# A mixing and gated feed-forward kernel on one core: reordered opening, 94-row gathers, cosines from the absolute phase, and layer 2 of the first chunk begun early

## The chip, the core and the metric

The kernel runs on one core of one Trainium2 chip. A time is the device time of one execution in microseconds (us). Of several executions the median is given, with the range or the number of runs where it matters. PE is the matmul engine, PEld its weight loads, DVE the vector engine, ACT the scalar (activation) engine, POOL the GpSimd engine, and SP the engine that issues most plain transfers.

## The reference

```python
x: (8, 3008, 256) float32            # batch, sequence, width
X = np.fft.fft(np.fft.fft(x, axis=1), axis=2).real      # mixing
t = X.reshape(24064, 256)
out = (gelu(t @ w_gate) * (t @ w_val)) @ w_out          # 256 -> 1536 -> 256, exact GELU
```

## The kernel before

The sequence of 3008 is factored into 94 x 32, and 3008 = 47 x 64 is used on the output side. For each batch the kernel adds and subtracts mirrored rows of `x` ("folds"), multiplies by a table G of cosines and sines (`s1`, into the tile A), reorders into a tile Z (`ch`, for later batches by way of device memory: SP writes `z` and reads it back), and multiplies Z by a second small table TP (`tp_e`, `tp_o`). The result is the input of the feed-forward part. It has chunks of up to 512 tokens, three for each batch. Layer 1 of a chunk takes 12 steps, one for each 128 hidden units, and I call a step a *slot*: 8 batches x 3 chunks x 12 make 288 slots. Layer 2 of a chunk is cut into 24 pieces of four matmuls, two pieces in each slot of the *next* chunk.

The mirrored rows come by gathers (indirect DMA) that POOL issues, with a column of row indices. Of 96 rows only 94 are used. Two rows have no meaning, and their index is only made legal:

```python
NP, NPX, NJ = 94, 96, 17

def cast_mirror(b, j0, nj):
    i0, o, idx = (16, 0, idx_0) if j0 == 0 else (17 - j0 - nj, 33 - j0 - nj, idx_x)
    gather(_sub(xb[b], [[1, nj * C]], (NJ + i0) * C),
           ap_replace(x, ap=[[32 * C, B * NP], [1, 32 * C]]), idx[:NPX, :], (b * T + o) * C)

def index_consts(i):                                   # idx = max(base - p, 0), by way of float32
    idx, base = ((idx_x, NP - 1), (idx_0, NP))[i]
    nc.gpsimd.iota(col_i[:, i : i + 1], pattern=[[0, 1]], base=base, channel_multiplier=-1, **IOTA)
    if i:
        nc.gpsimd.memset(col_i[0:1, i : i + 1], 0.0)
    nc.gpsimd.tensor_scalar(idx, col_i[:, i : i + 1], 0.0, None, op0=ALU.max)
```

`load_mirror` is the same for batches 2 to 7, in float32 and into the tile `x_raw`. The opening computes the tables on DVE and ACT while PE runs matmuls without use (`warm`) to raise its clock:

```python
warm(11); vec_consts(); g_phases(); vec_fills(); cw_phases()
g_sin(9, 7); g_sin_ends(); g_sin(1, 8); cw_sin()
t_columns(); t_phases(); t_sin(); warm(10)
...
fold_piece(9, 4); stage1(2); warm(4); fold_piece(13, 4); ...      # the first batch, ends in the first gate
```

And this is how a slot issues its work:

```python
pend = list(works[i // NFC - 1])           # at the first slot of a chunk: the 24 layer-2 pieces of the chunk before
...
parts["G"][fc]()                           # gate matmuls, Gelu on ACT
before[0]["g"][before[1]]()                # second gate matmul of the slot before (mirrored tokens)
parts["V"][fc]()                           # value matmul
pend.pop(0)()                              # a layer-2 piece
before[0]["v"][before[1]]()                # second value matmul; DVE and POOL write h = gelu * value
pend.pop(0)()                              # a layer-2 piece
```

POOL writes `h` for the mirrored tokens ("sign 1"), DVE for the others.

## Time and profile before

| | before |
|---|---|
| median time in the runs beside the changed kernel | 633.55 us (632.54 to 635.35, 4 runs) |
| profiled span | 632.1 us |
| first Gelu | 21.52 us |
| PE idle from 45 us on | two waits of over 0.5 us (0.63 at 52.8 us, 0.76 at 236.4 us) |

The busy table by windows, before, for 95 to 120 us (columns: length, then busy us of PE, PEld, DVE, ACT and POOL with counts, then granted clock, DMA share and GB/s):

```profile
95.00:120.00 25.00, 25.00 (x173) 16.54 (x171) 23.79 (x38) 18.00 (x35) 24.15 (x23) 1.00 0.50 132
```

PE has no idle time there at all. So a gain must come from the first slice of 16 us, or from the few waits later on. POOL is nearly as full as PE in that window (24.15 of 25).

The gathers of the kernel before in the view of DMA issues (count, median us from issue to landing):

```profile
x_raw<-in_x_dram,idx POOLq DMA_INDIRECT x18, 6.5
xb<-in_x_dram,idx POOLq DMA_INDIRECT x8, 4.9
```

Four rows of the timeline (start, duration, what ran, and in brackets the idle time before it and what ended it):

```profile
4.26 1.68 POOL L158 DMA_INDIRECT xb<-in_x_dram,idx  x1 [0.29 <-POOL idx L268]
10.02 0.19 DVE L216 TENSOR_TENSOR eo_sb<-x_stage,xb 94x8 bf16<-94x8 f32 x1 [0.89 <-DMA xb<-in_x_dram,idx]
21.52 0.60 ACT L638 ACTIVATE gelu_sb<-ps_g 128x512 bf16<-128x512 f32 x1 [1.10 <-PE ps_g L622]
52.77 0.28 PE L695 MATMUL ps_o<-Wo_sb,h_sb 128*128 128x256 bf16 x1 [0.63 <-POOL h_sb L671]
```

The first gather is issued at 4.26 us, and the first fold waits 0.89 us for it. At 52.77 us, in slot 14, PE waits 0.63 us for POOL's `h`.

### The profile page before, as it was taken

How to read it: one execution, taken by the hardware profiler on the slowest of the kernel's cores; microseconds unless marked ns; L12 is line 12 of the kernel's file. 1: busy time of each engine (PE TensorE's matmuls, PEld its weight loads, DVE VectorE, ACT ScalarE, POOL GpSimd, SP SyncE). 2: the span in 40 equal slices, each digit the busy share in tenths (PEclk: the TensorE clock that was granted, in tenths of full speed). 3: DMA queues.
4: the chain of work that ended last, by engine and by line, in shares of the span. 5: the costliest groups of instructions: out<-in, count | busy, mean ns of one | idle time of the engine just before them, and what ended most of it. 6: DMA issues, size and time to landing. Idle time of an engine off the chain costs nothing.

```text
span 632.1 us, 13032 instructions
## 1 busy us (share of the span) xinstructions
PE 618.9 (98%) x4285; PEld 407.4 (64%) x4285; DVE 580.9 (92%) x937; ACT 432.7 (68%) x855; POOL 505.7 (80%) x511
## 2 busy tenths in 40 slices
PE   7999999999999999999999999999999999999997
PEld 3446666666666666666666666666666666666666
DVE  7698889999899989999999999999999999999992
ACT  6787777666766667666776767766776766666651
POOL 8599799989997998879998799968988555555651
PEclk8999999999999999999999999999999999999999
DMA  8931925535454352633635325633222232221123
GB/s 152 179 61 26 250 63 147 139 99 138 121 146 107 91 140 65 167 84 100 156 93 155 93 66 138 153 92 104 57 53 57 75 104 54 52 51 38 43 51 80
DMA packets 51994, 63.84 MB, mean 101 GB/s; under 512 B 7783, under 2 KB 47194, under 8 KB 49530
## 3 DMA queue, kind: packets, MB, share of 16 engines
q1 hardware_dynamic: 45238, 47.23, 28.9%
q0 software_dynamic: 6096, 15.29, 11.5%
q8 instruction: 33, 0.54, 0.3%
q10 hardware_dynamic: 592, 0.49, 0.3%
q14 instruction: 35, 0.29, 0.1%
HBM read 38.86 MB, written 29.38 MB: 108 GB/s over the span
## 4 chain that ended last, share of the span: by engine, by line
PE 87%; DMA 4%; DVE 3%; POOL 2%; ACT 2%; issue 1%; POOLq 0%; DVEq 0%; ACTq 0%
PE ps_o L695 36%; PE ps_g L622 27%; PE ps_v L622 17%; DMA Z_sb<-z 3%; PE ps_dft L508 2%; PE ps_dft L544 2%; POOL h_sb L671 1%; DVE v_sb L669 1%; DMA xb<-in_x_dram,idx 1%; DVE h_sb L667 1%; PE ps_o L757 1%; PE ps_dft L574 1%; ACT gelu_sb L638 1%; DVE ve_sb L656 1%; PE ps_g L695 0%
## 5 line engine op out<-in xcount | busy, mean ns | idle before, releaser
L671 POOL TENSOR_TENSOR h_sb<-gelu_sb,v_sb 128x512 bf16<-128x512 bf16 (+1 forms) x288 | 328.7, 1144 | 106.3 <-DVE v_sb L669 92.0
L695 PE MATMUL ps_o<-Wo_sb,h_sb 128*128 128x256 bf16 (+1 forms) x2232 | 334.9, 273 | 1.0 <-POOL h_sb L671 1.0
L695 PEld LDWEIGHTS <-h_sb 128*128 128x128 bf16 (+1 forms) x2304 | 228.8, 100 | 112.5 <-POOL h_sb L671 2.7
L656 DVE SCALAR_TENSOR_TENSOR ve_sb<-EB_sb,yw,ps_v 128x512 f32<-128x512 bf16 (+1 forms) x288 | 212.1, 737 | 32.8 <-PE ps_v L622 29.0
L638 ACT ACTIVATE gelu_sb<-ps_g 128x512 bf16<-128x512 f32 (+1 forms) x288 | 169.6, 589 | 96.4 <-PE ps_g L622 93.0
L622 PE MATMUL ps_g<-EO_sb,W_sb 128*128 128x512 bf16 (+1 forms) x864 | 231.2, 375 | 2.7 <-ACT gelu_sb L647 2.0
L622 PE MATMUL ps_v<-EO_sb,W_sb 128*128 128x512 bf16 (+1 forms) x576 | 214.4, 375 | 0.5 <-ACT W_sb L423 0.5
L667 DVE TENSOR_TENSOR h_sb<-gelu_sb,ps_v 128x512 bf16<-128x512 bf16 (+1 forms) x288 | 195.0, 677 | 1.1 <-ACT gelu_sb L647 0.7
L669 DVE SCALAR_TENSOR_TENSOR v_sb<-ve_sb,ps_v 128x512 f32<-128x512 f32 (+1 forms) x288 | 192.6, 669 | 0.0
L622 PEld LDWEIGHTS <-W_sb 128*128 128x128 bf16 x1440 | 136.8, 98 | 82.3 <-issue 4.2
L647 ACT ACTIVATE gelu_sb<-ps_g 128x512 bf16<-128x512 f32 (+1 forms) x288 | 169.1, 587 | 0.0
L714 ACT ACTIVATE out_sb<-ps_o 128x512 f32<-128x512 f32 x92 | 54.9, 597 | 36.1 <-PE ps_o L695 36.0
L224 POOL TENSOR_TENSOR eo_sb<-ab_sb 94x512 bf16<-94x512 f32 (+1 forms) x60 | 66.6, 1110 | 0.1
L554 ACT ACTIVATE EO_sb<-ps_dft 128x512 bf16<-128x512 f32 (+1 forms) x44 | 26.0, 590 | 22.5 <-PE ps_dft L544 20.5
L511 ACT ACTIVATE S_sb<-ps_dft 96x512 bf16<-96x512 f32 x48 | 28.2, 587 | 11.3 <-PE ps_dft L508 11.3
L217 POOL TENSOR_TENSOR ab_sb<-x_raw,x_raw 94x508 f32<-94x508 f32 (+1 forms) x30 | 33.0, 1101 | 0.0
L220 POOL TENSOR_TENSOR ab_sb<-x_raw,x_raw 94x508 f32<-94x508 f32 (+1 forms) x30 | 32.9, 1096 | 0.0
L158 POOL DMA_INDIRECT x_raw<-in_x_dram,idx x18 | 17.0, 945 | 2.8 <-issue 0.6
L508 PE MATMUL ps_dft<-eo_sb,G 94*96 94x256 bf16 x102 | 19.2, 274 | 0.0
L544 PE MATMUL ps_dft<-TP,Z_sb 128*128 128x128 bf16 (+1 forms) x188 | 18.2, 218 | 0.5 <-DVE Z_sb L496 0.5
L544 PEld LDWEIGHTS <-Z_sb 128*128 128x128 bf16 x192 | 14.5, 98 | 2.4 <-DVE Z_sb L496 0.7
L757 PE MATMUL ps_o<-gelu_sb 128*128 128x512 bf16 x32 | 11.1, 498 | 1.2 <-DVE col L305 1.2
(128 smaller groups left out, 173.5 us busy)
## 6 DMA issues: line engine op xcount, KB each, us to landing
out_dram<-out_sb SPq DMA_DIRECT2D x361, 64.0 KB
x_raw<-in_x_dram SPq DMA_DIRECT2D x10, 768.0 KB
Z_sb<-z SPq DMA_DIRECT2D x6, 768.0 KB
z<-S_sb SPq DMA_DIRECT2D x6, 576.0 KB
EB_sb<-yrow SPq DMA_DIRECT2D x14, 128.0 KB
x_raw<-in_x_dram SPq DMA_DIRECT2D x2, 640.0 KB
z<-S_sb SPq DMA_DIRECT2D x6, 192.0 KB
EB_sb<-yrow SPq DMA_DIRECT2D x7, 120.2 KB
```

The lines of the kernel that those rows point to most:

```text
L217: eng.tensor_tensor(ab(0, 1, up), fwd(1, up), mir(255, down), op=ALU.add)
L224: eng.tensor_tensor(_sub(eo, [[C, nj], [1, 128]], j0 * C + g * 128), ab(0, 0, [[1, 128]]), ab(1, 0, [[1, 128]]), op=op)
L544: nc.tensor.matmul(ps[:, o : o + n], st["Z"][:, pair, g * 128 : g * 128 + 128], _sub(TP, [[1, n]], g * 128), start=True, stop=True)
L622: nc.tensor.matmul(ps[:, :n], W[nm, part][:, fs], src, start=start, stop=stop, **kw)
L638: nc.scalar.activation(gl[:, 0, :n], pg[:, :n], AF.Gelu)
L647: nc.scalar.activation(_sub(gl, [[-1, n]], TOK + n - 1), pg[:, :n], AF.Gelu)
L656: nc.vector.scalar_tensor_tensor(ve[:, :n], EB_bufs[b][:, c0 : c0 + n], yw[:, fc : fc + 1], pv[:, :n], op0=ALU.mult, op1=ALU.add)
L667: nc.vector.tensor_tensor(st["h"][:, fc, 0, :n], gl[:, 0, :n], pv[:, :n], op=ALU.mult)
L669: nc.vector.scalar_tensor_tensor(_sub(vv, [[-1, n]], n - 1), ve[:, :n], 2.0, pv[:, :n], op0=ALU.mult, op1=ALU.subtract)
L671: nc.gpsimd.tensor_tensor(st["h"][:, fc, 1, :n], gl[:, 1, :n], vv[:, :n], op=ALU.mult)
L695: nc.tensor.matmul(pso[:m, half], st["h"][:, fc, sign, h0 : h0 + m], Wo_sb[:, fc, :], start=(fc == 0), stop=(fc == NFC - 1),)
L714: nc.scalar.activation(_sub(osb, [[1, 2 * C]], 0, part_num=m), pso[:m, :], AF.Copy)
```

## The change

Its intent is a shorter opening and an earlier layer 2:

- gathers start sooner: row indices are made directly as integers, without the float detour, for 94 rows instead of 96; four more `j` columns of the forward `x` come by a casting DMA;
- cosines are taken from |phase|, so DVE has half as many phases to reduce; several phase computations move from DVE to ACT;
- the copy for the mirrored gate weights ("minus") and a weight cast move behind the chain to the first gate;
- the opening's warm-up `warm(11)` goes (32 warm-up matmuls become 20);
- the first layer-2 block of chunk 0 is issued in chunk 0's own slots.

```diff
@@ gathers (load_mirror the same)
-            _sub(xb[b], [[1, nj * C]], (NJ + i0) * C),
-            ap_replace(x, ap=[[32 * C, B * NP], [1, 32 * C]]), idx[:NPX, :], (b * T + o) * C)
+            _sub(xb[b], [[1, nj * C]], (NJ + i0) * C, part_num=NP),
+            ap_replace(x, ap=[[32 * C, B * NP], [1, 32 * C]]), idx[:NP, :], (b * T + o) * C)
@@ index_consts
-        nc.gpsimd.iota(col_i[:, i : i + 1], pattern=[[0, 1]], base=base, channel_multiplier=-1, **IOTA)
+        nc.gpsimd.iota(idx[:NP, :], pattern=[[0, 1]], base=base, channel_multiplier=-1)
         if i:
-            nc.gpsimd.memset(col_i[0:1, i : i + 1], 0.0)
-        nc.gpsimd.tensor_scalar(idx, col_i[:, i : i + 1], 0.0, None, op0=ALU.max)
+            nc.gpsimd.memset(idx[0:1, :], 0)
@@ phases: three examples of DVE -> ACT
-        nc.vector.tensor_scalar(cf[:, 0:128], row_c, col_n0, 0.25, op0=ALU.mult, op1=ALU.add)
+        nc.scalar.activation(cf[:, 0:128], row_c, AF.Copy, scale=col_n0)
-        nc.vector.tensor_copy(parc, ps[:, 0:5])
+        nc.scalar.activation(parc, ps[:, 0:5], AF.Copy)
-            nc.vector.tensor_scalar(
-                tf[:, i * K1 : (i + 1) * K1], k1, parc[:, 0:1], parc[:, 1 + i : 2 + i], op0=ALU.mult, op1=ALU.add)
+            nc.scalar.activation(
+                tf[:, i * K1 : (i + 1) * K1], k1, AF.Identity, scale=parc[:, 0:1], bias=parc[:, 1 + i : 2 + i])
@@ opening (cut)
-        warm(11)
...
-        warm(10)
...
+        warm(14)
         fold_piece(9, 4)
@@ layer 2
+                first = (b, ci, sub) == (0, 0, 0)
...
-                        start=(fc == 0),
+                        start=(fc == 0 and not (first and sign)),
                         stop=(fc == NFC - 1),
+                        skip_group_check=first,
@@ slots
+        first = works[0]
+        sooner = {6: [first[0]], 7: [first[3]], 10: [first[1]], 11: [first[4]], 13: [first[2], first[5]]}
+        works[0] = first[6:]
...
+            two = sooner.pop(i, []) if i <= NFC + 1 else [pend.pop(0) for _ in range(2) if pend]
```

The changed `start` is needed because the two signs share one bank of PSUM (the memory that matmuls write to) and are now interleaved. The Trainium skill (PSUM — Partial Sum Buffer, "Terms") says that a matmul which starts an accumulation clears the written-bits of the whole bank it writes to, in the groups of 32 partitions that it writes. So only the first of the two may start. The experiments with this edit (e1, e9, e10, e11) gave correct results, which agrees; no run here lets both start.

More of the change, by code (lines that the diff above doesn't have):

```diff
@@ L99, in stage_tile @@
     def stage_tile():
-        return work([NPX, 9, C], FP32, "h", 2, "x_stage")
+        return work([NPX, 5, C], FP32, "h", 2, "x_stage")
     eo = const_pool.tile([NP, NJ, 2, 128], BF16, name="eo_sb")
@@ L165, in load_mirror @@
         gather(
-            _sub(raw_tile(MIRROR), [[1, nj * C]], i0 * C),
-            ap_replace(x, ap=[[32 * C, B * NP], [1, 32 * C]]), idx[:NPX, :], (b * T + o) * C)
+            _sub(raw_tile(MIRROR), [[1, nj * C]], i0 * C, part_num=NP),
+            ap_replace(x, ap=[[32 * C, B * NP], [1, 32 * C]]), idx[:NP, :], (b * T + o) * C)
     def load_part(b, k):
@@ L186, in cast_mirror @@
         gather(
-            _sub(xb[b], [[1, nj * C]], (NJ + i0) * C),
-            ap_replace(x, ap=[[32 * C, B * NP], [1, 32 * C]]), idx[:NPX, :], (b * T + o) * C)
+            _sub(xb[b], [[1, nj * C]], (NJ + i0) * C, part_num=NP),
+            ap_replace(x, ap=[[32 * C, B * NP], [1, 32 * C]]), idx[:NP, :], (b * T + o) * C)
     def fold_ops(b, j0, nj, eng):
@@ L194, in fwd @@
         def fwd(c0, pat):
-            if b == 0 and j0 not in range(1, 9):
-                return _sub(stage[0], [[C, nj]] + pat, (j0 - 9 if j0 else 8) * C + c0, part_num=NP)
+            if b == 0 and j0 in (9, 0):
+                return _sub(stage[0], [[C, nj]] + pat, (j0 - 9 if j0 else 4) * C + c0, part_num=NP)
             if half:
@@ L234 @@
     col_p, col_h, col_a, col_n0, col_e = (const_pool.tile([128, 1], FP32, name=f"col{i}") for i in range(5))
-    sc_g = const_pool.tile([128, 2], FP32)
+    sc_g, bi_g = (const_pool.tile([128, 2], FP32, name=f"g_{i}") for i in ("scale", "bias"))
+    quarter = const_pool.tile([128, 1], FP32)
     row_j = const_pool.tile([128, NJ], FP32)
@@ L239 @@
     par = const_pool.tile([1, 5, 128], FP32)
-    one = const_pool.tile([1, 1], FP32)
+    one = const_pool.tile([1, 2], FP32)
     parc = const_pool.tile([128, 5], FP32)
@@ L254 @@
     idx_x, idx_0 = (const_pool.tile([128, 1], mybir.dt.uint32, name=f"idx{i}") for i in range(2))
-    col_i = const_pool.tile([128, 2], FP32)
     IOTA = dict(allow_small_or_imprecise_dtypes=True)
@@ L274, in pool_consts, with pool_consts2, par_n1 @@
         nc.gpsimd.memset(row_k[:, NK - 1 : NK], 0.0)
+    def pool_consts2():
         nc.gpsimd.iota(row_c, pattern=[[1, 128]], base=0, channel_multiplier=0, **IOTA)
-    def pool_consts2():
-        nc.gpsimd.iota(
-            par[:, 0, :], pattern=[[1, 16], [0, 2], [32, 2], [0, 2]], base=1, channel_multiplier=0, **IOTA)
+        nc.gpsimd.iota(par[:, 0, :], pattern=[[1, 16], [0, 8]], base=1, channel_multiplier=0, **IOTA)
+        nc.gpsimd.iota(row_t, pattern=[[1, K1]], base=0, channel_multiplier=0, **IOTA)
+    def par_n1():
+        nc.vector.tensor_scalar(
+            _sub(par, [[4, 32], [1, 2]], 2), _sub(par, [[4, 32], [1, 2]], 2), 32.0, None, op0=ALU.add)
         for r, v in ((120, 0.0), (122, 32.0), (126, 16.0)):
-            nc.gpsimd.memset(par[:, 0, r : r + 2], v)
-        nc.gpsimd.iota(row_t, pattern=[[1, K1]], base=0, channel_multiplier=0, **IOTA)
+            nc.vector.memset(par[:, 0, r : r + 2], v)
     def vec_fills():
@@ L289, in vec_fills @@
         nc.vector.memset(G[:, 16, 0 : 2 * NK], 0.0)
-        nc.vector.memset(one, 1.0)
+        nc.vector.memset(one[:, 1:2], 1.0 / K1)
+        nc.vector.memset(quarter, 0.25 * TWO_PI)
         nc.vector.memset(one_h, 1.0)
@@ L307, in vec_consts, with vec_consts2, magnitude @@
         nc.vector.scalar_tensor_tensor(col_h, col_a, -2.0, col_p, op0=ALU.mult, op1=ALU.add)
-        nc.vector.tensor_scalar(col_e, col_h, -1.0, 1.0, op0=ALU.mult, op1=ALU.add)
+        nc.vector.tensor_scalar(col_n0, col_p, 1.0 / C, None, op0=ALU.mult)
         nc.vector.tensor_scalar(sc_g[:, 1:2], col_h, -TWO_PI, None, op0=ALU.mult)
         nc.vector.tensor_scalar(sc_g[:, 0:1], col_h, TWO_PI, -TWO_PI, op0=ALU.mult, op1=ALU.add)
+    def vec_consts2():
+        nc.vector.tensor_scalar(bi_g[:, :], sc_g[:, :], -0.25, None, op0=ALU.mult)
+        nc.vector.tensor_scalar(col_e, col_h, -1.0, 1.0, op0=ALU.mult, op1=ALU.add)
+        nc.vector.tensor_scalar(keep2, col_p, 1.0, -2.0, op0=ALU.min, op1=ALU.mult)
+    def magnitude(a, d):
+        nc.scalar.activation(a, d, AF.Abs)
     def g_phases():
-        f, r, d = (_sub(t, [[1, 2 * NGP]], 0, part_num=NP) for t in (ff, rr, rd))
+        f, r, d = (_sub(t, [[1, NGP + NK]], NGP - NK, part_num=NP) for t in (ff, rr, rd))
         nc.vector.scalar_tensor_tensor(
@@ L320, in g_phases @@
         )
-        nc.vector.tensor_scalar(f[:, NK:NGP], f[:, NGP + NK :], 0.25, None, op0=ALU.add)
-        nc.vector.tensor_scalar(f[:, 0:NK], f[:, NGP : NGP + NK], 0.125, None, op0=ALU.add)
+        nc.vector.tensor_scalar(f[:, 0:NK], f[:, NK : 2 * NK], 0.125, None, op0=ALU.add)
         reduced(d, r, f)
-    def g_sin(j0, nj):
-        for h in range(2):
-            nc.scalar.activation(
-                _sub(G, [[96, nj], [2 * NK, 2], [1, NK]], j0 * 96 + h * NK),
-                _sub(rd, [[NK, nj], [NGP, 2], [1, NK]], j0 * NK, part_num=NP),
-                AF.Sin, scale=sc_g[:NP, h : h + 1])
@@ L333, in g_sin_ends, with g_cos @@
-    def g_sin_ends():
-        nc.scalar.activation(
-            _sub(G, [[NK, 2], [1, NK]], 16 * 96 + 2 * NK), _sub(rd, [[NGP, 2], [1, NK]], 16 * NK, part_num=NP),
-            AF.Sin, scale=sc_g[:NP, 0:1])
-        for h in range(2):
-            nc.scalar.activation(
-                _sub(G, [[1, NK]], h * NK), _sub(rd, [[1, NK]], 0, part_num=NP),
-                AF.Sin, scale=sc_g[:NP, h : h + 1])
+    def g_cos(dst, j0, nj, h):
+        nc.scalar.activation(
+            _sub(G, [[96, nj], [1, NK]], dst), _sub(ff, [[NK, nj], [1, NK]], j0 * NK, part_num=NP),
+            AF.Sin, scale=sc_g[:NP, h : h + 1], bias=bi_g[:NP, h : h + 1])
@@ new lines, in g_sin, with g_rows @@
+    def g_sin(dst, j0, nj, h):
+        nc.scalar.activation(
+            _sub(G, [[96, nj], [1, NK]], dst), _sub(rd, [[NK, nj], [1, NK]], NGP + j0 * NK, part_num=NP),
+            AF.Sin, scale=sc_g[:NP, h : h + 1])
+    def g_rows(j0, nj):
+        for h in range(2):
+            g_sin(j0 * 96 + (2 + h) * NK, j0, nj, h)
+        if j0 == 9:
+            magnitude(_sub(ff, [[1, NGP]], 0, part_num=NP), _sub(rd, [[1, NGP]], NGP, part_num=NP))
+        for h in range(2):
+            g_cos(j0 * 96 + h * NK, j0, nj, h)
@@ L342, in cw_phases, with g_ends @@
+    def g_ends():
+        g_cos(16 * 96 + 2 * NK, 16, 1, 0)
+        g_sin(16 * 96 + 3 * NK, 16, 1, 0)
+        for h in range(2):
+            g_sin(h * NK, -1, 1, h)
     def cw_phases():
-        nc.vector.tensor_scalar(col_n0, col_p, 1.0 / C, None, op0=ALU.mult)
-        nc.vector.tensor_scalar(cf[:, 0:128], row_c, col_n0, 0.25, op0=ALU.mult, op1=ALU.add)
-        nc.vector.tensor_scalar(cf[:, 128:256], row_c, col_n0, 0.5, op0=ALU.mult, op1=ALU.add)
-        reduced(cd[:, :], cr[:, :], cf[:, :])
+        nc.scalar.activation(cf[:, 0:128], row_c, AF.Copy, scale=col_n0)
+        reduced(cd[:, 0:128], cr[:, 0:128], cf[:, 0:128])
+        magnitude(cf[:, 128:256], cd[:, 0:128])
@@ L348, in cw_sin @@
     def cw_sin():
-        nc.scalar.activation(_sub(CW, [[256, 2], [1, 128]], 0), cd[:, :], AF.Sin, scale=-TWO_PI)
+        nc.scalar.activation(CW[:, 0, 0, :], cf[:, 128:256], AF.Sin, scale=-TWO_PI, bias=quarter)
+        nc.scalar.activation(CW[:, 1, 0, :], cd[:, 0:128], AF.Sin, scale=TWO_PI)
     def cw_rest():
@@ L370, in t_columns @@
         for i in range(5):
-            nc.tensor.matmul(ps[:, i : i + 1], par[:, i, :], one, start=True, stop=True)
-        nc.vector.tensor_copy(parc, ps[:, 0:5])
-        nc.vector.tensor_scalar(parc[:, 0:1], parc[:, 0:1], 1.0 / K1, None, op0=ALU.mult)
+            nc.tensor.matmul(ps[:, i : i + 1], par[:, i, :], one[:, int(i == 0) : int(i == 0) + 1], start=True, stop=True)
+        nc.scalar.activation(parc, ps[:, 0:5], AF.Copy)
     def t_phases():
@@ L377, in t_phases @@
         for i in range(2):
-            nc.vector.tensor_scalar(
-                tf[:, i * K1 : (i + 1) * K1], k1, parc[:, 0:1], parc[:, 1 + i : 2 + i], op0=ALU.mult, op1=ALU.add)
+            nc.scalar.activation(
+                tf[:, i * K1 : (i + 1) * K1], k1, AF.Identity, scale=parc[:, 0:1], bias=parc[:, 1 + i : 2 + i])
         reduced(td[:, :], tr[:, :], tf[:, :])
@@ L392, with sin_table @@
     sink = const_pool.tile([1, 1], BF16, name="sink")
+    def sin_table():
+        nc.scalar.activation(dump, one[:, 0:1], AF.Sin)
     def gelu_table():
@@ L404, in load_wo @@
     def load_wo(q):
-        n = NFC // 4
+        n = NFC // 2
         nc.gpsimd.dma_start(
@@ L409, in load_wo, with make_w @@
                 moe_w_out, ap=[[C, 128], [128 * C, n], [1, C]], offset=moe_w_out.offset + q * n * 128 * C))
-    def make_w(i, f0, n, parts=(0, 1), engine="A"):
+    def make_w(i, f0, n, parts=(0, 1), engine="A", m_at=None):
         def run():
@@ L426, in run, with minus @@
             if i == 0 and 1 in parts:
-                nc.scalar.activation(W["g", "M"][:, f0 : f0 + n], ps[:, m - n : m], AF.Copy, scale=keep2)
+                def minus():
+                    nc.scalar.activation(W["g", "M"][:, f0 : f0 + n], ps[:, m - n : m], AF.Copy, scale=keep2)
+                if m_at is None:
+                    minus()
+                else:
+                    m_at.append(minus)
         return run
@@ L732, in opening @@
         xb[0] = xb_tile(0)
-        for j0, nj, at in ((9, 8, 0), (0, 1, 8)):
+        for j0, nj, at in ((9, 4, 0), (0, 1, 4)):
             nc.sync.dma_start(
@@ L736, in opening @@
                 in_=ap_replace(x, ap=[[32 * C, NPX], [1, nj * C]], offset=x.offset + j0 * C))
+        cast_forward(0, 13, 4)
         pool_consts()
-        pool_consts2()
         index_consts(0)
@@ L741, in opening @@
         cast_forward(0, 1, 8)
+        pool_consts2()
         cast_mirror(0, 5, 4)
-        cast_mirror(0, 1, 4)
         index_consts(1)
         cast_mirror(0, 0, 1)
-        for f0, n in ((0, 256), (256, 256), (512, 1024)):
+        cast_mirror(0, 1, 4)
+        for f0, n in ((0, 256), (256, 256), (512, 512), (1024, 512)):
             load_w(f0, n)
-        for q in range(4):
+        for q in range(2):
             load_wo(q)
         idle = gelu_tile()[:, 0, :]
+        nc.vector.memset(one[:, 0:1], 1.0)
+        sin_table()
         nc.vector.memset(idle, 0.0)
@@ L761, in fold_piece @@
                 f()
-        def stage1(jg):
-            s1(0, jg, 0)()
-            s1(0, jg, 1, "V" if jg == 0 else "A")()
-        warm(11)
+        vec_fills()
         vec_consts()
         g_phases()
-        vec_fills()
+        vec_consts2()
+        g_rows(9, 7)
         cw_phases()
-        g_sin(9, 7)
-        g_sin_ends()
-        g_sin(1, 8)
+        g_ends()
+        g_rows(1, 8)
+        par_n1()
+        t_columns()
         cw_sin()
-        t_columns()
         t_phases()
         t_sin()
-        warm(10)
-        nc.vector.tensor_scalar(keep2, col_p, 1.0, None, op0=ALU.min)
-        nc.vector.tensor_scalar(keep2, keep2, -2.0, None, op0=ALU.mult)
         gelu_table()
@@ L785, in opening @@
         cw_rest()
+        warm(14)
         fold_piece(9, 4)
-        stage1(2)
-        warm(4)
+        s1(0, 2, 0)()
         fold_piece(13, 4)
+        s1(0, 2, 1, "V")()
+        warm(5)
         fold_piece(5, 4)
-        warm(2)
-        stage1(1)
-        warm(3)
+        s1(0, 1, 0)()
+        s1(0, 1, 1)()
         fold_piece(0, 1)
-        stage1(3)
-        warm(2)
-        fold_piece(3, 2)
-        fold_piece(1, 2)
-        stage1(0)
-        make_w(0, 0, 256, engine="V")()
+        s1(0, 3, 0)()
+        warm(1)
+        fold_piece(1, 4)
+        s1(0, 3, 1, "V")()
+        s1(0, 0, 0)()
+        s1(0, 0, 1, "V")()
+        minus = []
+        make_w(0, 0, 256, m_at=minus)()
         ch(0, 0)()
         ch(0, 1, "V")()
-        make_w(1, 0, 256, engine="V")()
         tp_e(0, 0)()
         tp_o(0, 0, "V")()
+        make_w(1, 0, 256, engine="V")()
+        minus[0]()
     def behind_first_gate():
@@ L918, in feed @@
             parts["V"][fc]()
-            if pend:
-                pend.pop(0)()
+            if two:
+                two.pop(0)()
             for f in pool.pop(i, []):
@@ L924, in feed @@
                 before[0]["v"][before[1]]()
-            if pend:
-                pend.pop(0)()
+            if two:
+                two.pop(0)()
             for f in fill.pop(i, []):
```

## The prediction

> **What bounds it now.** Time 633.96 us. The per-slice busy table shows PE at 99% from about 45 us on (25.00 of 25.00 us busy in 95 to 120); the chain of waits is 87% PE. Only earlier arrival there wins. Only the opening has slack: first gate matmul at 20.47 us, second at 21.11, first Gelu at 21.52 (timeline). From 20.4 to 45.4 DVE (21.5 of 25 us) and ACT (21.2) set the pace, PE does about 19.6 us of matmul work (counts times the 0.217 us spacing).
>
> **Opening, before.** ACT starts the sines at 4.96, does t_sin at 8.91, reloads the table, evacuates the first A at 13.42. DVE starts folding at 10.02, having waited for the mirror gather (issued 4.26); the last fold ends at 15.53. Then Z waits behind ACT's minus copy (0.47) and DVE's W cast (0.68).
>
> **What changes.**
> 1. The gather is issued near 2.5 us instead of 4.26, so x for the first fold lands near 7 to 8 us. The folds no longer wait for it.
> 2. ACT goes from 9 to 21 phase activations. From the trace, starts are about 0.1 us + columns/1200 apart, 0.08 more with a vector scale. First sine at about 4.7; cosines cost an Abs of 408 columns (0.44); DVE round trips for the small phases 0.9 and 0.6; t_phases 0.5. t_sin starts at about 11.6 (was 8.91), A evacuation at about 16 (was 13.4). DVE's reduction for t sits in order ahead of the folds, so folds start at about 11.6, later than 10.02. Folds are cheaper (13..16 in bf16: 0.85 instead of 1.28).
> 3. The minus copy and second W cast leave the chain to the gate: about 0.6 to 1.1 us won back. Net, first Gelu at about 21.5, unchanged within 1.5 us.
> 4. Layer 2: four pieces (0.44 us each) enter slots 6 to 11, where PE has slack. But the last piece of the first block (sign 1, fc 8..11) comes in slot 13. It needs POOL's product for fc 11, and POOL is saturated from 33.15 to 52.7 us (0.31 idle), its order unchanged. Before, PE met it in slot 14 and waited 0.63. Now PE reaches it about 4 us early and stands with slot 14's matmuls (1.09 us) and slot 13's fills (0.6) undone behind it. Loss: about 1.7 us, never regained.
>
> Sum: 0 from the opening, +1.7, which gives 635.7; a tuned order may pay where I do not see it, so I shade down: **634.6 us, range 630.0 to 638.5. Faster by over 2%: 0.01; within 2%: 0.94; slower by over 2%: 0.05.**
>
> **What would show it.** Right: ACT busy without gaps from 5 to 18 us; first fold after 11 us, waiting for ACT and not DMA; a PE idle of 2.5 to 4 us near 48 to 52 us released by POOL h; PE solid afterwards. Wrong: folds before 10 us; first Gelu before 20 us; no such PE idle.
>
> **What would make it wrong.** ACT faster than that spacing: up to 2 us won. PE cold: the Trainium skill (TensorE: Matmul & The Clock Gate, Part 1) says about 3.4 us of matmuls must precede full clock; here the first warm-up matmuls were 0.43 us apart, later 0.23. With t_columns now first, 14 warm-ups could run cold and hold the first s1 until 14 us. Gathers now have 94 rows, not 96: the skill (DMA: Bandwidth & Descriptors, "Why a DMA increments its semaphore by 16 and not by 1") says a transfer is spread over the largest divisor up to 16; 94 would give 2 engines. No run here shows it for gathers; if so, the opening grows by over 10 us.

## More of the kernel before

From the profile page of the kernel before: the line of busy times by engine, PE's busy tenths in 40 equal slices, two of the DMA queues (packets, MB, share of 16 engines) and the chain of waits by engine.

```profile
PE 618.9 (98%) x4285; PEld 407.4 (64%) x4285; DVE 580.9 (92%) x937; ACT 432.7 (68%) x855; POOL 505.7 (80%) x511
PE   7999999999999999999999999999999999999997
q0 software_dynamic: 6096, 15.29, 11.5%
q8 instruction: 33, 0.54, 0.3%
PE 87%; DMA 4%; DVE 3%; POOL 2%; ACT 2%; issue 1%; POOLq 0%; DVEq 0%; ACTq 0%
```

## The result

The changed kernel took **684.84 us (683.76 to 686.22, 4 runs), against 633.55 us**. The ratio is 1.0807, with a 95% interval of 1.0774 to 1.0841. Here and below a ratio is the mean time of one kernel's fast runs over that of the other's of the same rounds, so it is not quite the ratio of the medians. The kernel is about 51 us slower, and the prediction of 634.6 us was wrong.

The same lines of the page, after:

```profile
PE 622.6 (91%) x4224; PEld 410.4 (60%) x4273; DVE 579.3 (85%) x934; ACT 437.0 (64%) x867; POOL 518.2 (76%) x507
PE   4595891999999999998999999999999999999997
q0 software_dynamic: 20800, 15.31, 10.2%
PE 71%; DMA 15%; issue 5%; POOL 5%; ACT 2%; DVE 1%; SPq 1%; POOLq 0%; ACTq 0%; DVEq 0%
```

PE's work is unchanged (622.6 us busy against 618.9), but it has holes in the first seven slices, that is in the first 120 us. (The 24 PE instructions fewer of the change show in PEld, 4273 against 4285, and 12 matmuls less. The count of 4224 matmuls is lower still because some records are missing from the trace.) The software queue moved the same 15.3 MB with 20,800 packets instead of 6,096. The chain of waits now holds 15% DMA.

```profile
100.00:120.00 20.00, 5.01 (x30) 3.02 (x29) 3.68 (x6) 3.01 (x7) 6.58 (x7) 0.66 0.19 73
```

In 100 to 120 us, where PE was saturated before, it is busy for 5.01 us. All five engines are mostly idle, and so is the DMA: a share of 0.19 of 16 engines, about 3 of them. The granted TensorE clock, 1.00 before, is 0.66 on average in this stretch. An idle machine with DMA nearly idle too looks odd for a wait on a transfer. It fits a transfer that uses few of the 16 engines.

The gathers after, in the view of DMA issues:

```profile
x_raw<-in_x_dram,idx POOLq DMA_INDIRECT x18, 21.5
xb<-in_x_dram,idx POOLq DMA_INDIRECT x8, 14.8
```

They took three times as long to land. Two pieces of the chain of waits, after (start, length, what):

```profile
3.06 18.48 DMA xb<-in_x_dram,idx
39.32 18.35 DMA xb<-in_x_dram,idx
```

Four rows of the timeline, after:

```profile
3.06 1.94 POOL L158 DMA_INDIRECT xb<-in_x_dram,idx  x1 [0.32 <-POOL idx L265]
21.55 0.19 DVE L216 TENSOR_TENSOR eo_sb<-x_stage,xb 94x8 bf16<-94x8 f32 x1 [8.50 <-DMA xb<-in_x_dram,idx]
113.42 0.21 POOL L216 TENSOR_TENSOR ab_sb<-x_raw,x_raw 94x8 f32<-94x8 f32 x1 [15.90 <-DMA x_raw<-in_x_dram,idx]
116.02 0.39 PE L724 MATMUL ps_o<-Wo_sb,h_sb 128*128 128x256 bf16 x1 [13.05 <-POOL h_sb L699]
```

The gather was issued 1.2 us earlier than before, but its data came at 21.5 us. At 113 us the later half of the story is seen: POOL's fold of batch 2 waits 15.90 us for an `x_raw` gather. POOL's products for `h` come behind that fold in the program and in the trace, and PE waits 13.05 us for them. The trace has the granted clock at 0.50 from 106.4 to 123.4 us, so PE also works at half the clock for some time after this wait.

The delay grows in steps. Compared with the kernel before, the gate's Gelu starts 11.32 us later in slot 0, 21.3 in slots 12 and 13, 39.83 in slot 28 and 49.91 in slot 276 (counted through the Gelus in both traces). A slow gather thus costs three times: in the opening, at batch 1 and at batch 2. For later batches the loads are issued early enough to hide, but near 300 us the chain of waits holds three stores of the output, the longest of them

```profile
273.07 18.36 DMA out_dram<-out_sb
```

and PE waits up to 2.5 us (at 320.44 us) for the output buffers that those stores hold. The kernel before has no such wait. e2 below has it too (1.2 us at 317.23), and e1 doesn't, so it belongs to the 94-row gathers. That the stores queue behind the gathers on the same few DMA engines is likely, but no run separates it.

### The profile page after: what moved, and what is told of

Read it like the earlier page. It is cut to its first block, busy times and chain, and to the rows that moved or that the text cites. A ratio compares the mean times of both kernels' runs of the same rounds, so it can differ in the third digit from the quotient of the medians.

```text
span 682.0 us, 12965 instructions
## 1 busy us (share of the span) xinstructions
PE 622.6 (91%) x4224; PEld 410.4 (60%) x4273; DVE 579.3 (85%) x934; ACT 437.0 (64%) x867; POOL 518.2 (76%) x507
## 3 DMA queue, kind: packets, MB, share of 16 engines
q0 software_dynamic: 20800, 15.31, 10.2%
## 4 chain that ended last, share of the span: by engine, by line
PE 71%; DMA 15%; issue 5%; POOL 5%; ACT 2%; DVE 1%; SPq 1%; POOLq 0%; ACTq 0%; DVEq 0%
PE ps_o L724 29%; PE ps_g L650 21%; PE ps_v L650 14%; DMA out_dram<-out_sb 6%; DMA xb<-in_x_dram,idx 5%; DMA Z_sb<-z 3%; POOL h_sb L699 3%; PE ps_dft L536 1%; PE ps_dft L572 1%; SPq L644 1%; DVE v_sb L697 0%; PE ps_dft L602 0%; ACT gelu_sb L666 0%; ACT gelu_sb L675 0%; POOL eo_sb L220 0%
## 5 line engine op out<-in xcount | busy, mean ns | idle before, releaser
L724 PE MATMUL ps_o<-Wo_sb,h_sb 128*128 128x256 bf16 (+1 forms) x2232 | 337.6, 274 | 22.3 <-POOL h_sb L699 19.3
L650 PE MATMUL ps_v<-EO_sb,W_sb 128*128 128x512 bf16 (+1 forms) x576 | 216.7, 379 | 0.5 <-ACT W_sb L445 0.5
L539 ACT ACTIVATE S_sb<-ps_dft 96x512 bf16<-96x512 f32 x48 | 28.2, 588 | 11.7 <-PE ps_dft L536 11.6
L158 POOL DMA_INDIRECT x_raw<-in_x_dram,idx x18 | 27.1, 1508 | 3.5 <-POOL h_sb L699 1.7
L216 POOL TENSOR_TENSOR ab_sb<-x_raw,x_raw 94x8 f32<-94x8 f32 (+1 forms) x30 | 6.3, 209 | 15.9 <-DMA x_raw<-in_x_dram,idx 15.9
L572 PEld LDWEIGHTS <-Z_sb 128*128 128x128 bf16 x192 | 14.5, 98 | 3.1 <-DVE Z_sb L524 0.9
```

Source lines behind the costliest of these rows:

```text
L572: nc.tensor.matmul(ps[:, o : o + n], st["Z"][:, pair, g * 128 : g * 128 + 128], _sub(TP, [[1, n]], g * 128), start=True, stop=True)
L650: nc.tensor.matmul(ps[:, :n], W[nm, part][:, fs], src, start=start, stop=stop, **kw)
L724: nc.tensor.matmul(pso[:m, half], st["h"][:, fc, sign, h0 : h0 + m], Wo_sb[:, fc, :], start=(fc == 0 and not (first and sign)), stop=(fc = ...
```

## The experiments

Theory A is that the 94-row gathers are the cause: they are spread over 2 DMA engines and not 16, as the last lines of the prediction feared. The rivals were the opening (a longer ACT chain, a cold PE), the layer-2 order, and, for the row count, a general penalty for any number that is not a multiple of 16.

### e1: the change with 96-row gathers

```diff
-        _sub(xb[b], ..., part_num=NP), ..., idx[:NP, :]      (both gathers)
+        _sub(xb[b], ...), ..., idx[:NPX, :]
     def index_consts(i):
+        nc.gpsimd.memset(idx, 0)
```

> The changed kernel with its mirror gathers back at 96 rows (index rows 94 and 95 set to 0), all else changed. Theory A (the row count alone lost the 51 us: 94 rows go over 2 DMA engines): the time returns to the region of the kernel before, 630 to 638 us; the first gather lands within 6 us of its issue instead of 18.5, and no wait of POOL for x_raw of 15.9 us remains. My recorded sum for everything else was +1.7 us, so 634 to 637. Rival B (the new order of the opening and of layer 2 lost most of it): stays above 660 us.

Measured: 643.26 us beside 634.41 for the kernel before, ratio 1.0163 (1.0135 to 1.0190). Against the change's 1.0807 this one edit gives back 0.0644, or 41 us of the 51. That refutes rival B. But I had expected 634 to 637 us and at most 638, and 643 is above that. The view of DMA issues of e1:

```profile
x_raw<-in_x_dram,idx POOLq DMA_INDIRECT x18, 6.5
xb<-in_x_dram,idx POOLq DMA_INDIRECT x8, 3.5
```

The landing times are no longer than in the kernel before (6.5, and 3.5 against 4.9). 1.6% remain, and e4 to e14 look for them.

### e2 and e3: the kernel before with 94 and with 95 rows

```diff
-            _sub(xb[b], [[1, nj * C]], (NJ + i0) * C), ..., idx[:NPX, :]      (both gathers)
+            _sub(xb[b], [[1, nj * C]], (NJ + i0) * C, part_num=94), ..., idx[:94, :]     # e3: 95
```

> The kernel before with nothing changed but 94 instead of 96 rows in the gathers. Theory A: slower by 35 to 60 us (668 to 695), first gather landing about 15 to 19 us after issue, x_raw gathers at 20 us or more in the median (6.5 before). Rival B: within 5 us of the kernel before.

> The kernel before with 95-row gathers. Theory A in its divisor form (largest divisor of the row count up to 16: 96 gives 16 engines, 95 gives 5, 94 gives 2): x_raw gathers land in about 8 to 10 us in the median (estimate: 760 KB over 5 engines at the 25 GB/s per busy engine that the changed kernel shows, and 2 to 3 us of latency), total 635 to 645 us. Rival A2 (any row count that is not a multiple of 16 breaks the gather into many small packets, which is what costs): 95 is as slow as 94, landing 20 us or more, total 668 to 695.

Measured: e2 677.94 us, ratio 1.0695 (1.0671 to 1.0720); e3 649.25 us, ratio 1.0243 (1.0219 to 1.0266). The DMA issues of e2, then of e3:

```profile
x_raw<-in_x_dram,idx POOLq DMA_INDIRECT x18, 21.9
xb<-in_x_dram,idx POOLq DMA_INDIRECT x8, 14.2
```

```profile
x_raw<-in_x_dram,idx POOLq DMA_INDIRECT x18, 12.0
xb<-in_x_dram,idx POOLq DMA_INDIRECT x8, 7.7
```

Two rows less, with everything else unchanged, cost the kernel before 44 us. So the row count alone makes most of the loss: 44 of some 51 us here, and 41 by e1. The order 96, 94, 95 in landing time (6.5, 21.9 and 12.0 us) is not an order of size. It is the order of the largest divisor up to 16: 16, 2 and 5. This is the rule of the Trainium skill (DMA: Bandwidth & Descriptors, "Why a DMA increments its semaphore by 16 and not by 1"), and these runs agree with it for gathers, which no run had shown before. The rival "every count that is no multiple of 16 is equally bad" fails on e3. The packets themselves show the number of engines. In gathers of 8192-byte rows that had no other gather beside them, mostly two such packets were in flight at once with 94 rows (e2 at 418.90 us: 14.0 of 16.9 us), mostly four or five with 95 (e3 at 390.62 us: 6.5 of 8.3 us), and 13 to 16 for most of the time with 96 (before at 183.10 us: 2.9 of 4.3 us). The many added packets of the software queue are another possible rival. They are of 4 bytes: 674 in that gather of e2 against 16 in that of before. They were in flight in only 1.2 of the 16.9 us, while the two large packets went on, so they are not what costs. My own figures for e3 were missed by a little: I had written 635 to 645 us and a landing of 8 to 10 us.

Why the loss is less than the engines' ratio of 8 shows in the records of single packets. An 8192-byte packet of a gather took 496 ns when 16 engines were working and 309 ns when 2 were, so an engine moves 16.5 GB/s in company and 26.5 GB/s nearly alone. An estimate from these: 94 rows of 8192 bytes over 2 engines at 26.5 GB/s need 14.5 us, over 16 at 16.5 GB/s 2.9 us. The gathers of e2 and of the kernel before that are named above took 16.9 and 4.3 us from their first packet to their last. In e2 4.5 us passed before the first packet (1.8 in before), and about 0.5 us after the last one in both. POOL also spends longer issuing a 94-row gather: 1.51 us against 0.95.

### e4: e1 with the old layer-2 order

```diff
-        sooner = {6: [first[0]], ..., 13: [first[2], first[5]]}
-            two = sooner.pop(i, []) if i <= NFC + 1 else [pend.pop(0) for _ in range(2) if pend]
+            two = [pend.pop(0) for _ in range(2) if pend]      (start and skip_group_check as before, too)
```

> The changed kernel with 96-row gathers and with layer 2 of the first chunk in its old slots (from slot 12). My step 4 on record (the piece in slot 13 waits for POOL, 1.7 us lost): faster than the run with 96 rows and the new layer 2 by 1 to 2.5 us, and the PE idle before the first layer-2 block ends shrinks from 2.5 to 4 us to under 1. Rival C (moving layer 2 into slots with PE slack pays): slower than it by 1 to 2.5 us.

Measured: 640.80 us, ratio 1.0107 (1.0087 to 1.0127). Against e1 of the same rounds this is 2.5 us by medians and 3.6 by ratios. PE's waits in slots 13 and 14 in e1:

```profile
52.82 0.28 PE L725 MATMUL ps_o<-Wo_sb,h_sb 128*128 128x256 bf16 x1 [1.07 <-POOL h_sb L700]
55.04 0.39 PE L725 MATMUL ps_o<-Wo_sb,h_sb 128*128 128x256 bf16 x1 [1.94 <-POOL h_sb L700]
```

The same stretch in e4:

```profile
55.12 0.28 PE L724 MATMUL ps_o<-Wo_sb,h_sb 128*128 128x256 bf16 x1 [0.65 <-POOL h_sb L700]
```

The pieces placed in slot 13 need POOL's products, which come no earlier than before. PE keeps to the order of the program here and stands in front of them for 3.0 us in all instead of 0.65. The wait has a second cost: the granted clock fell to 0.50 from 54.4 to 57.8 us in e1 (from 56.2 to 59.6 us in e10 below), where it is 1.00 in e4 and e5. In e1 the lag of the gate's Gelu behind the kernel before grows from 2.00 us in slot 13 to 6.74 in slot 14, and part of it is regained later; in e4 it stays at 2.34.

### e5 and e6: the number of warm-up matmuls

e4 is still 1% slower than the kernel before, although its first Gelu comes only 2.15 us late. In its trace the lag *grows* late in the run, from 3.67 us in slot 28 to 6.23 in slot 276, where the code of the two kernels is the same. Four waits there, 3.5 us together, are PE waiting for the read of Z. Before these reads SP issues stores of the output, and in e4 23 of SP's 480 DMA issues take over 1.0 us, against 5 before; 22 of the 23 coincide with one of the 33 transfers of 16 KB in the queue q8 of kind "instruction" (on the page above: 33 packets, 0.54 MB). The Trainium skill (Runtime: NRT & Kernel Launch, "Instruction fetch mechanics") says that an engine's instructions come by DMA in blocks of 16 KiB, 256 instructions. 33 blocks of 256 are 8448, which fits PE's count in the kernel before (4285 matmuls and 4285 weight loads on the page) and none of the other engines' counts there. Between two of these transfers PE runs about 256 matmuls and weight loads (median 256 in the kernel before). The change has 24 PE instructions fewer, because it runs 12 warm-up matmuls fewer. Theory F: the number of PE instructions sets when those fetches happen, and where they meet SP's stores they delay them.

```diff
 e5 = e4 +
+        warm(12)
         vec_fills()
 e6 = before +
-        warm(11)
...
-        warm(10)
+        warm(9)
```

> The run with 96 rows and the old layer 2, with 12 warm-up matmuls more at the very start, where PE idles until 8.4 us anyway; PE has then as many instructions as in the kernel before (the change has 24 fewer). Theory F: of the 6.4 us still lost, about 4 come from where PE's instruction fetches (queue of kind instruction, 33 of them, one per about 18 us) fall: with 24 instructions fewer nearly every fetch starts together with a store issue of SP, which then takes 1.0 to 1.9 us instead of 0.6 (22 such stalls against 5 before), and the loads and the Z reads behind it come late. It expects 636.0 to 638.0 us, at most 8 store issues over 1 us, PE's waits for Z back under 0.3 us, first Gelu at 23 to 23.7. Rival (the stalls come from the shifted phase of the DMA traffic itself): stays at 639.5 to 641.5, over 15 such store issues.

> The kernel before with its first 11 warm-up matmuls and one later one removed, nothing else. Theory F: first Gelu within 0.5 us of the kernel before, and yet 2 to 5 us slower in total (636 to 639), with over 15 SP store issues of more than 1 us at the fetch times and PE waits for Z of 0.5 us and more. Rival: no difference beyond the opening, under 1 us.

Measured, beside 632.98 us for the kernel before: e5 635.23 us, ratio 1.0033 (1.0018 to 1.0048), so 12 *more* useless matmuls made e4 some 4.7 us faster, and more than I expected (636.0 to 638.0). e6 took 636.00 us, ratio 1.0046 (1.0031 to 1.0062), though its first Gelu came 0.78 us sooner than before. SP's slow issues: 3 in e5, 20 in e6. SP's queue ahead of a late Z read in the kernel before:

```profile
504.61 2.41 SPq L616 DMA_DIRECT2D out_dram<-out_sb  x4
507.13 0.52 SPq L530 DMA_DIRECT2D Z_sb<-z  x1
```

The same in e4, where a fetch falls at 510.9 us, and one of the four stores, issued at 510.79, takes 1.85 us instead of 0.6:

```profile
509.61 3.67 SPq L645 DMA_DIRECT2D out_dram<-out_sb  x4
513.39 0.53 SPq L559 DMA_DIRECT2D Z_sb<-z  x1
```

What PE's matmuls on Z waited for, over the whole run (us, times), before, in e4 and in e6:

```profile
  DMA Z_sb<-z: 0.5, 2
```

```profile
  DMA Z_sb<-z: 3.5, 4
```

```profile
  DMA Z_sb<-z: 2.9, 4
```

The Z reads are the one visible place where the delay becomes PE time. They do not cover all of it: e4's late loads for batch 2 also left a wait of 1.64 us for POOL at 84.6 us (0.32 before).

### e7 and e8: what is left in the opening

e7 puts three small phase computations of e5 back on DVE. e8 goes from the other side: the phases of the kernel before, with the change's new `x` order (96 rows) and its order of the opening's end.

```diff
 e7 = e5 +
-        nc.scalar.activation(cf[:, 0:128], row_c, AF.Copy, scale=col_n0)
+        nc.vector.tensor_scalar(cf[:, 0:128], row_c, col_n0, None, op0=ALU.mult)
-        nc.scalar.activation(parc, ps[:, 0:5], AF.Copy)
+        nc.vector.tensor_copy(parc, ps[:, 0:5])
-            nc.scalar.activation(tf[...], k1, AF.Identity, scale=..., bias=...)
+            nc.vector.tensor_scalar(tf[...], k1, ..., op0=ALU.mult, op1=ALU.add)
 e8 = before + new order of x and of the opening's end (cut), g_phases, t_phases, cw_phases as before
```

> As the run with 12 warm-ups more, with the CW phase, the copy of the t columns and the t phases back on DVE; the cosines from the absolute phase stay on ScalarE. My step 2 on record (the chain through ScalarE holds t_sin, the table reload, the A evacuations, and through DVE's order the folds): t_sin at 10.5 to 11.5 us instead of 12.8, folds from 9 to 10.5 instead of 12.6, first A evacuation at about 15.2 instead of 17.3, first Gelu at 21.2 to 22.2 instead of 23.6; total 1.2 to 2.5 us below the run with 12 warm-ups. Rival (x's arrival or PE's cold clock holds the opening): first Gelu stays above 23.

> A version meant to beat both: the kernel before with its phases on DVE and ScalarE as they were, 96-row gathers with the index straight from the iota, the change's x order (gather first, rows 13 to 16 by casting DMA), and the change's order of the end of the opening (A evacuations shared, W copies after Z). Layer 2 as before, the same number of PE instructions as before. My reading expects folds from 9.2 us, A evacuations from 13.4, first Gelu at 19.3 to 20.3 (21.5 before) and 631.5 to 633 us, 0.2 to 0.4 per cent below the kernel before. If x still arrives at 10 us: no gain.

Measured: e7 633.16 us, ratio 0.9999 (0.9982 to 1.0017); e8 632.92 us, ratio 0.9992 (0.9973 to 1.0011). Both tie with the kernel before. In total time e7 gains 2.1 us on e5, as expected (though its first Gelu, 22.84 us, missed the 21.2 to 22.2 that I had written), so the move of those phases to ACT did cost about 2 us. In the trace of e1, which has them on ACT, the first fold and the first Gelu come at:

```profile
12.60 0.19 DVE L216 TENSOR_TENSOR eo_sb<-x_stage,xb 94x8 bf16<-94x8 f32 x1
23.57 0.60 ACT L667 ACTIVATE gelu_sb<-ps_g 128x512 bf16<-128x512 f32 x1 [1.12 <-PE ps_g L651]
```

The fold is not waiting for `x` here (no bracket): it waits its turn behind the phases on DVE, which wait for ACT. In e7 it starts at 9.35 us.

The expectation of e8 failed in its mechanism: its first Gelu came at 22.13 us, not 19.3 to 20.3. PE in e8:

```profile
6.02 2.29 PE L370 MATMUL ps_v<-one,par 1*128 1x1 f32 x10
8.24 4.45 PE L763 MATMUL ps_o<-gelu_sb 128*128 128x512 bf16 x10
12.48 0.53 PE L472 MATMUL ps_g<-G,eo_sb 94*128 94x96 bf16 x4
```

Ten warm-ups take 4.45 us (2.33 in the kernel before) and hold the first real matmul until 12.48 us, though the folds had begun at 10.25 us. They start 0.42 to 0.43 us apart in e8 and 0.21 to 0.22 in the kernel before. The clock record of e8 first shows 1.00 at 13.9 us, that of the kernel before at 5.1. So these warm-ups ran at the low clock and became the obstacle. The Trainium skill (TensorE: Matmul & The Clock Gate, Part 1) calls the warm-up "run-variable", because the window that decides on the clock runs freely. e7 and e11 below, whose openings are the same code, show the variation, though not its reason. Their first Gelus come at

```profile
22.84 0.60 ACT L667 ACTIVATE gelu_sb<-ps_g 128x512 bf16<-128x512 f32 x1 [1.95 <-PE ps_g L651]
```

and

```profile
21.11 0.60 ACT L667 ACTIVATE gelu_sb<-ps_g 128x512 bf16<-128x512 f32 x1 [1.12 <-PE ps_g L651]
```

The granted clock differs too: from 17.0 to 23.6 us it was 0.50 in e7 and 1.00 in e11 (which had 0.50 from 8.2 to 11.5 us instead). So one trace of the opening is good to about 1.7 us. Claims on it must rest on the timed rounds, and those say that neither order of the opening beats the old one.

### e9, e10 and e11: the layer-2 order once more

e9 is the kernel before with the early layer 2, its last pieces in slots 14 and 15. e10 is e1 with the 12 warm-ups of e5, so that only the layer-2 order separates it from e5. e11 is e7 with the order of e9: the change with everything repaired.

```diff
 e9 (e11 the same on e7)
+        sooner = {6: [first[0]], 7: [first[3]], 10: [first[1]], 11: [first[4]], 14: [first[2]],
+                  15: [first[5], first[6]]}
+        works[0] = first[7:]                                  (the loop that issues them: cut)
 e10 = e1 +
+        warm(12)
```

> The kernel before with layer 2 of the first chunk begun early as in the change, but its last two fc groups in slots 14 and 15 instead of both in slot 13; number of TensorE instructions as before. If step C (the early order is not bad in itself, only the group placed in slot 13 waits for POOL) holds: no PE wait of over 0.4 us for POOL's h near 47 to 56 us, and 631.5 to 633 us, ratio 0.996 to 1.000. Rival (beginning layer 2 inside the chunk's own slots delays the later layer-1 work by itself): over 634 us.

> The change with 96-row gathers and 12 warm-ups more; only the layer-2 order differs from e5. If the cost of the layer-2 order (2.5 us, e1 against e4) and that of the missing TensorE instructions (4.7 us, e4 against e5) are independent: e5 plus 2 to 3 us, so 637.3 to 638.5, with fewer than 8 SP DMA issues of over 1 us. Rival (the 2.5 us was also a matter of where the instruction fetches fall): within 0.8 us of e5.

> The change repaired: 96-row gathers, 12 warm-ups back, small phases on DVE, and layer 2 of the first chunk early but with the last groups in slots 14 and 15. e7 without the early layer 2 tied with the kernel before. Expected 0.5 us either side of e9, or 631.5 to 633; if it is over 634, the early layer 2 costs something that e9 doesn't show.

Measured, beside 633.62 us: e9 633.90 us, ratio 1.0007 (0.9994 to 1.0019); e10 639.44 us, ratio 1.0092 (1.0079 to 1.0105); e11 633.68 us, ratio 1.0006 (0.9993 to 1.0019). e10 less e5 is 3.7 us by ratios, a little over the 2 to 3 that I expected and the same as e1 less e4. With few slow SP issues in e10 (4), the layer-2 loss and the fetch loss are independent. PE's waits in e10 are those of e1:

```profile
53.38 0.28 PE L725 MATMUL ps_o<-Wo_sb,h_sb 128*128 128x256 bf16 x1 [1.04 <-POOL h_sb L700]
55.60 0.28 PE L725 MATMUL ps_o<-Wo_sb,h_sb 128*128 128x256 bf16 x1 [1.93 <-POOL h_sb L700]
```

e9 misses its range by 0.9 us and e11 by 0.7. The wait for POOL is gone, but PE has found three others:

```profile
52.01 0.27 PE L544 MATMUL ps_dft<-TP,Z_sb 128*128 128x128 bf16 x2 [0.91 <-DVE Z_sb L496]
54.79 0.60 PE L696 MATMUL ps_o<-Wo_sb,h_sb 128*128 128x256 bf16 x4 [0.82 <-ACT out_sb L716]
62.81 1.03 PE L696 MATMUL ps_o<-Wo_sb,h_sb 128*128 128x256 bf16 x8 [0.64 <-ACT out_sb L716]
```

In the last two, layer 2 has one PSUM tile, and the next block waits until ACT has emptied it. The first is a wait for DVE's copy into Z. The old order had something else in between. So the early layer 2 can be made harmless, but it does not gain: there was only 0.63 us of waiting to win in slot 14, and a saturated PE has no gap to fill.

### e12, e13 and e14: which fetches cost

Theory F allows a forecast: take the fetch times from the trace of the kernel before, shift them by the time of n PE instructions, and count how many fall on an SP issue. For 48 instructions more it gave 26 of 33.

```diff
 e12 = before, after warm(10):
+        for _ in range(24):
+            nc.tensor.matmul(ps[:, 0:1], idle[:, 0:128], idle[:, 0:1], start=True, stop=True)
 e13 = e6 with 12 such matmuls of one column;   e14 = before with warm(3) for warm(11)
```

> The kernel before with 24 matmuls of one column (48 TensorE instructions) added in an idle stretch of the opening; first Gelu expected within 0.5 us of before. Shifting the instruction fetches in the trace of before by 48 TensorE instructions (about 3.4 us earlier) makes 26 of 33 fetches fall on an SP store issue, against 6 as it is. Theory F (each such meeting lengthens an SP issue, and the late Z reads stall PE): 15 to 25 SP issues of over 1 us against 5, PE waits for Z of 0.4 us and more, and 635 to 637.5 us. Rival (it is the number of warm-ups, the PE's warmth or its start that counted in e5 and e6): more warm-ups don't hurt, 632 to 633.5 us, at most 8 SP issues of over 1 us.

> e6 (12 warm-ups fewer than before, 636.0 us though its first Gelu came 0.78 us sooner) with 12 matmuls of one column in an idle stretch of the opening. Theory (the number of TensorE instructions sets which bursts of SP issues ahead of Z reads meet an instruction fetch): no PE wait for Z of over 0.3 us, and 632.5 to 634 us beside a before of 633.5, that is ratio 0.998 to 1.001. Rival (the 11 warm-ups before the phases matter as work or warmth): stays at ratio 1.003 to 1.006.

> The kernel before with 3 warm-ups instead of 11 at its start, so 16 TensorE instructions fewer. Shifting the fetches of before by 16 instructions makes them meet 1 of the 6 bursts ahead of Z reads (5 of 6 at 20 and more). Theory: at most one PE wait for Z of over 0.4 us, ratio 0.997 to 1.002. Rival (each missing warm-up costs its part of what e6 lost): two thirds of e6's loss, ratio 1.003 to 1.004.

e12 had its 16 slow SP issues, as forecast, but took 634.14 us, ratio 1.0012 (0.9999 to 1.0026), and its forecast time of 635 to 637.5 was missed. A slow issue of stores does not matter by itself. In e12 they fall on other stores, for example here, with a `yrow` exchange behind them (another small one by way of device memory) and no Z read. PE waits for Z for more than 0.15 us only once in the whole run (0.24 us):

```profile
443.31 3.41 SPq L616 DMA_DIRECT2D out_dram<-out_sb  x4
446.83 0.52 SPq L588 DMA_DIRECT2D EB_sb<-yrow  x1
```

So I narrowed the theory: what counts is whether a fetch falls into the burst of SP issues that ends in a Z read. There are six such bursts. In the traces a fetch meets none of them before and in e5, one in e12, and five in e4 and in e6. e13 and e14 test this. e13, with the instruction count restored by matmuls that take next to no time, took 632.37 us beside 633.31, ratio 0.9989 (0.9969 to 1.0009). It has no wait for Z of over 0.15 us and meets no burst. e6 had lost 0.46% at the same work, so the count matters and not the warmth. The first Gelus of the two are 0.14 us apart (20.74 and 20.88), so a shift of the whole opening is not what separates them. For e14 I forecast one meeting and a tie. It took 635.06 us, ratio 1.0020 (1.0000 to 1.0041), and its trace shows five bursts met and four waits for Z (0.46, 0.68, 0.52 and 0.99 us). The forecast of one meeting was wrong: the count in the trace of before jumps from 1 to 5 between 16 and 20 instructions, and by e14's own trace the jump lies 4 to 8 instructions nearer to before than e14, that is at 8 to 12. Counted by the whole length of a fetch, about 1 us, and not by its start, the trace of before gives five meetings from 8 instructions on, so the way of counting has a part in this miss. That Z was waited for where the bursts were met supports the theory. The total of e14 alone does not decide: its interval runs from no loss to more than the 1.003 to 1.004 that the rival of its expectation forecast, and it is e13 that speaks against that rival. That the meetings can be forecast only to some 10 instructions (0.7 us) limits its use. What fetch and store issue share on the chip stays open: no run here separates it.

## Why the prediction was wrong

The budget of the loss, as a chain of ratios in which each kernel differs from the next by one thing (each ratio is to the kernel before in the same rounds; the rounds ran on different chips):

| step | ratios to before | cost |
|---|---|---|
| 94 instead of 96 rows | 1.0807 -> 1.0163 (after, e1) | 41 us |
| 24 PE instructions fewer | 1.0163 -> 1.0092 (e1, e10) | 4.5 us |
| layer-2 pieces in slot 13 | 1.0092 -> 1.0033 (e10, e5) | 3.7 us |
| small phases on ACT | 1.0033 -> 0.9999 (e5, e7) | 2.2 us |

(Costs are differences of ratios times about 634 us. The intervals of the ratios are 0.0013 to 0.0034 either way, so the first step is good to about 2.8 us, the second to 2.0 and the others to about 1.5.) Without the first row the prediction would still have missed: e1's 643.26 us lies above its range of 630.0 to 638.5. The other three rows make up that part.

1. **"The gather is issued near 2.5 us ..., so x for the first fold lands near 7 to 8 us. The folds no longer wait for it."** This is the step that failed. The gather was issued at 3.06, and the fold began at 21.55 after a wait of 8.50 us for it. The prediction charged the removal of two rows as nothing, and left the divisor rule of the skill, as one doubt among others, within the 5% that it gave to "slower by over 2%", with a harm limited to "the opening grows by over 10 us". The opening did grow by 11.3 us, but the same gathers also feed batches 1 and 2, where POOL waits for them in order and holds PE. With 96 rows (e1) the step was half right: the folds no longer waited for `x`, yet began later, at 12.60.
2. **The ACT chain.** The mechanism was right, the size too small. Predicted were t_sin at 11.6, folds at 11.6 and A at 16; e1 shows 12.78, 12.60 and 17.29. The net effect on the first Gelu was given as 0 within 1.5 us; it was +2.05 in e1, and 2.2 us of time between e5 and e7.
3. **The minus copy and the second W cast leave the chain.** They did, but e8, which has that order with the old phases, only ties. The 0.6 to 1.1 us were not seen as a gain; PE's cold warm-ups took that place in e8's trace.
4. **Layer 2 in slot 13.** It was right in place and cause. The term was mis-sized: 1.7 us predicted, 2.5 to 3.7 measured (e1 less e4, e10 less e5). The sum had only PE's idle time in it; the drop of the granted clock to 0.50 for 3.4 us after the wait was not in it. The runs do not separate the two parts. In the changed kernel itself this wait was buried under the gathers' waits.
5. **What the prediction did not contain:** the 24 PE instructions fewer. In the changed kernel's own trace too, fetches meet five of the six bursts ahead of Z reads, and PE waits 3.5 us for Z in four places. The prediction counted the missing warm-ups as an opening matter only; they cost 3 to 5 us (e6 against before, e1 against e10, e4 against e5) hundreds of microseconds later.
6. **"PE cold ... could hold the first s1 until 14 us."** It held it until 15.00 us in e1, where `t_columns` took 2.26 us (1.27 before) and 14 warm-ups 4.55 us. It belongs to the 2 us of point 2.

## What to carry to other kernels

Count the rows of every transfer when you "tidy" it, because rows that are loaded in vain can be what spreads it over all engines; and if a rule that you know says that an edit could make a transfer eight times narrower, cost that branch in full, at every place where the transfer is used. Moving work earlier in an engine's program helps only if its inputs come earlier too. In a saturated kernel, look at the instruction queue and at the issuing engine when a lag grows where the code is the same, as it did in e4. And timed rounds, not one trace, should judge changes of under 2 us in an opening.

## What the Trainium skill lacked or had wrong

- *DMA: Bandwidth & Descriptors*, "Why a DMA increments its semaphore by 16 and not by 1": it gives the divisor rule and an exception for some direct copies of the software queue, but does not name indirect gathers and so leaves open which holds for them. These runs show the rule: 16, 5 and 2 large packets in flight with 96, 95 and 94 rows, and median landing 6.5 us with 96 rows, 12.0 with 95 and 21.9 with 94; POOL's issue also grows, 0.95, 1.15 and 1.51 us; and the queue's packets rise from 6,096 to 10,544 and 20,176.
- The same page would gain from the rate of one engine in a gather: 26.5 GB/s with 2 engines at work and 16.5 with 16 (8192-byte packets, 309 and 496 ns).
- *Runtime: NRT & Kernel Launch*, "Instruction fetch mechanics" calls the cost of crossing a block "mostly hidden". Here it was hidden on PE itself, but a fetch that fell on an SP store issue lengthened that issue from 0.6 to between 1.0 and 1.9 us; 24 PE instructions fewer cost 0.46% (e6), and 12 matmuls of one column undid it (e13, 0.9989). No page mentions this.
- *TensorE: Matmul & The Clock Gate*, Part 1 gives about 3.4 us for the warm-up. In e8 PE ran 21 warm-ups and ten small matmuls from 1.21 us on, and the last warm-ups, at 12 us, still started 0.42 to 0.43 us apart, so as a plan for an opening with small matmuls in between the figure was too hopeful; that page's "run-variable" agrees with e7 and e11, whose same openings differ by 1.7 us.
